# An mLSTM cell and a SwiGLU block on one core: when the third piece of the weights is asked for, where the second pair's first state is summed, and who rounds block 1

## The chip, the cores and the metric

The kernel runs on one core of a Trainium2 chip. The metric is the device time of one execution in microseconds (us). The engines are PE (TensorE, with its weight loads written PEld), DVE (VectorE), ACT (ScalarE), POOL (GpSimd) and SP (SyncE). SP and ACT issue the DMAs: those of SP appear in the profile as queue q1, those of ACT as q10, and both are served by the core's 16 DMA engines.

## The reference, cut to what matters

Inputs have 4 batches, 8 heads, 768 tokens and 40 features. The cell's output, 3072 tokens by 320, goes through a gated feed-forward block with 1536 hidden features. The three weight matrices are float64 in memory.

```python
for t in range(S):
    m_new = np.maximum(f_gate[:, :, t] + m, i_gate[:, :, t])
    f_stab = np.exp(f_gate[:, :, t] + m - m_new)
    i_stab = np.exp(i_gate[:, :, t] - m_new)
    m = m_new
    C = f_stab * C + i_stab * np.einsum('bhd,bhe->bhde', vt, kt)
    n = f_stab * n + i_stab * kt
    y[:, :, t] = o * (C @ qt) / np.maximum(np.abs(n @ qt), 1.0)
...
g = x @ w_gate
silu = g * (1.0 / (1.0 + np.exp(-g)))
return (silu * (x @ w_val)) @ w_out
```

## The kernel before, in words

**Tiling.** The tokens are cut into six chunks of 128 per batch; a chunk of all four batches is a group of 512 tokens. The cell runs chunk by chunk in matrix form: scores, weights, values, and a state `C` carried on. Heads come in two halves P = 0 and P = 1 (two batches each). For the first chunk the weights of all heads lie in `W0`, which is a view of the first eight slots of `h_sb`, the 13-slot ring that later holds the hidden features (512 words a slot); batch u uses slots 2u and 2u + 1.

**Feed-forward.** For group g, `hidden(g, m)` makes block m of the 12 blocks of 128 hidden features: PE multiplies the gate and the value weights (line 648, 20 products in the profile) into two PSUM banks of tag "gen" (four banks in all, so two blocks are in flight), ACT takes Silu of the first (line 653), and DVE multiplies by the second into slot `(12g + m) mod 13` of `h_sb` (line 654). A block can only start on PE when DVE has finished line 654 of the block before the last. `project` then multiplies by the output weights.

**Weights.** They are float64 and arrive as pairs of 32-bit words, in ten pieces (`piece_load`, line 165): pieces 0 and 1 hold block 0 and block 1, pieces 2 to 6 two blocks each, pieces 7 to 9 the output weights. A piece of gate and value weights has a gate half, issued by SP, and a value half, issued by ACT for pieces 0 to 4 and by SP after that. A piece waits in a buffer: one of two `raw` buffers, or a tile that is free at the time ("home"). Block j is converted in three steps: `scale(j)`, two ACT operations (lines 190 and 192: `top`, `low`); `join(j)`, two DVE operations (lines 199 and 200); and `rounded(j)`, one integer addition on POOL or on DVE (line 207).

**Order.** Every engine runs its instructions in the order in which the kernel writes them. The opening part is written out by hand (`first_...`, lines 564 to 611), with `burn` issuing constant bfloat16 products on PE. Then a table `slots` says what runs after each block m of group 0, and a table `ahead` which blocks are converted inside `hidden(0, m)`, after its products have been issued and before its Silu. Blocks 9 to 11 are rounded by DVE, all others but block 0 by POOL.

**What the change touches.** In the opening: `sig(0)` and `sig(1)` (Sigmoid of the output gates, line 463), `piece_load(2)` into slots 8 to 12 of `h_sb`, `piece_load(3)` into `wo_sb`, `burn(6)`, `piece_load(4)` into a `raw` buffer, `first_state(0)`, `convert(1)` and the Exp of `step1` (line 609). In the group's table: `first_state(1)` (PE line 552, 32 products, and a copy into `C`, line 121) and the loads of the next `k` and `q` after block 0; `piece_load(6)` after block 1.

**What lies further down the same queues.** After block 2 SP issues `weights_load(1)`: two loads of the running maxima `M_dram` into `w_sb` (line 447). After block 6 come `weights_sub(1, P)` on DVE (line 451), which reads `w_sb`, and `weights_mask` on POOL (line 456). Inside `hidden(0, 7)`, block 10 is converted and rounded on DVE, before DVE's line 654 of block 7.

Of the kernel before, what the change touches and what calls it, by code (L numbers as in the profile page):

```python
# [13 lines left out]
AF = mybir.ActivationFunctionType  # L14
# [10 lines left out]
def kernel(  # L25
# [18 lines left out]
    nc = tc.nc  # L44
# [7 lines left out]
    D1 = D + 1  # L52
# [4 lines left out]
    NKC = DM // HP  # L57
    UH = BH // 2
    UA = UH // 2
    NH = NFC + 1  # L60
# [15 lines left out]
    def bank(name, tag="cell"):  # L76
        return psum.tile([128, 512], F32, name=name, tag=tag)

    def half(i):
        return slice(i * SUB, (i + 1) * SUB)  # L80
# [5 lines left out]
    def heads(P):  # L86
        return slice(P * UH, (P + 1) * UH)

    k_sb = const.tile([128, BH, DP], F32)
    q_sb = const.tile([128, BH, DP], F32)  # L90
# [10 lines left out]
    wo_sb = const.tile([128, NFC, DM], F32)  # L101
    h_sb = const.tile([128, NH, TW], F32)
# [16 lines left out]
    def copy(eng, dst, src):  # L119
        if eng is nc.scalar:  # L120
            nc.scalar.copy(dst, src)
        else:
            eng.tensor_copy(dst, src)
# [16 lines left out]
    def piece_load(p, home=None):  # L140
        kind, m, n = PIECES[p]
        if kind == "gv":
            a, d = NKC, n * 128
            src = [(slice(i * HP, (i + 1) * HP), w[:, m * 128:(m + n) * 128].rearrange("(c p) f -> p c f", p=HP))
                   for i, w in enumerate((moe_w_gate, moe_w_val))]
            queues = (nc.sync, nc.scalar if p < 5 else nc.sync)
        else:
            a, d = n, DM
            src = [(slice(0, 128), moe_w_out[m * 128:(m + n) * 128].rearrange("(a p) d -> p a d", p=128))]
            queues = (nc.sync,)  # L150
        if src[0][1].dtype == F32:
            for r, w in src:
                if kind == "o":
                    nc.sync.dma_start(out=wo_sb[r, m:m + n, :], in_=w)
                else:
                    for x in range(n):
                        nc.sync.dma_start(out=wgv_sb[r, m + x], in_=w[:, :, ts(x, 128)])
            return
        if home is None:
            raw = conv.tile([128, 4 * NKC * 128], U32, name="raw")  # L160
        else:
            raw = home.rearrange("p a t -> p (a t)").bitcast(U32)
        raw = raw[:, 0:2 * a * d]
        for (r, w), queue in zip(src, queues):
            queue.dma_start(out=raw[r].rearrange("p (a d) -> p a d", a=a), in_=w.bitcast(U32))
        words = raw.rearrange("p (a d two) -> p a d two", two=2, a=a)
        raws[p] = (words[:, :, :, 0], words[:, :, :, 1])
        split(p)
# [4 lines left out]
    def split(p):  # L173
        if p in raws:
            lo, hi = raws.pop(p)
            kind, m, n = PIECES[p]
            if kind == "gv":
                for c in range(n):
                    r = slice(c * 128, (c + 1) * 128)
                    blocks[m + c] = (lo[:, :, r], hi[:, :, r], wgv_sb[:, m + c])  # L180
            else:
                for c in range(0, n, 2):
                    blocks[NFC + (m + c) // 2] = (lo[:, c:c + 2], hi[:, c:c + 2], wo_sb[:, m + c:m + c + 2, :])

    def scale(j):
        if j in blocks:
            lo, hi, dst = blocks[j]
            a, d = hi.shape[1], hi.shape[2]
            top = conv.tile([128, NKC * 128], F32, name="top", bufs=1).rearrange("p (a d) -> p a d", a=a)
            nc.scalar.mul(top, hi.bitcast(F32), 2.0 ** -112)  # L190
            low = conv.tile([128, NKC * 128], I32, name="low").rearrange("p (a d) -> p a d", a=a)
            nc.scalar.mul(low, lo, 2.0 ** -29)
            blocks[j] = (low, top.bitcast(U32), dst)

    def join(j):
        if j in blocks:
            lo, top, dst = blocks[j]
            both = dst.bitcast(U32)
            nc.vector.tensor_scalar(both, top, scalar1=3, scalar2=None, op0=ALU.logical_shift_left)
            nc.vector.scalar_tensor_tensor(both, in0=top, scalar=0x80000000, in1=both, op0=ALU.bitwise_and,  # L200
                                           op1=ALU.bitwise_or)
            blocks[j] = (lo, dst.bitcast(I32))
# [6 lines left out]
    def convert(j, eng=None):  # L209
        scale(j)  # L210
        join(j)
        rounded(j, eng)
# [10 lines left out]
    warm = early.tile([128, 1], F32)  # L223
# [35 lines left out]
    step1 = keep1  # L259
# [81 lines left out]
        eng.tensor_tensor(vw_sb[:, heads(P)], v_sb[:, heads(P)], w_sb[:, heads(P), last].to_broadcast([128, UH, D1]),  # L341
                          op=ALU.mult)

    def small(name, n=UA):
        return bank(name)[:, 0:n * D1].rearrange("p (a d) -> p a d", d=D1)

    def add(n, P):
        ps = [small("add") for _ in range(2)]
# [8 lines left out]
    def state(s):  # L357
        return C_ring[s % 3]
# [103 lines left out]
    def sig(P):  # L462
        nc.scalar.activation(o_sb[:, heads(P)], o_sb[:, heads(P)], AF.Sigmoid)


    def burn(n, tag="cell"):
        t = bank("burn", tag)
        for _ in range(n):
            nc.tensor.matmul(t, lhsT=junk[:, 0:128], rhs=junk, start=True, stop=True)
# [4 lines left out]
    A, V, G = nc.scalar, nc.vector, nc.gpsimd  # L474
# [52 lines left out]
    def first_own(u):  # L527
        first_y[u] = bank("first_y", "gen")[:, 0:H * D1].rearrange("p (h d) -> p h d", d=D1)
        for h in range(H):
            nc.tensor.matmul(first_y[u][:, h, :], lhsT=W0[:, u * H + h, :], rhs=v_sb[:, u * H + h, :], start=True, stop=True)  # L530
# [13 lines left out]
            nc.vector.tensor_tensor(x, x, o_sb[:, u * H:(u + 1) * H], op=ALU.mult)  # L544
        nc.gpsimd.tensor_copy(x_sb[:, 2 * P:2 * P + 2, DM:], x_sb[:, 2 * P:2 * P + 2, 0:HP])

    def first_state(P, eng):
        ps = small("add")
        for a in range(UA):
            for two in range(2):  # L550
                h = P * UH + 2 * a + two
                nc.tensor.matmul(ps[half(two), a, :], lhsT=k_sb[:, h, :], rhs=vw_sb[:, h, :], start=True, stop=True)
        copy(eng, state(2)[:, P * UA:(P + 1) * UA], ps)

    def first_seam(P, engs):
# [30 lines left out]
    first_scores(1)  # L586
    first_x(1)
    sig(0)
    sig(1)
    piece_load(2, h_sb[:, NH - NKC:])  # L590
    piece_load(3, wo_sb)
    burn(3)
    first_own(2)
    first_own(3)
    first_gate(0)
    first_x(2)
# [1 line left out]
    first_seam(0, (A, A, V))  # L598
    scale(0)
    first_gate(1)  # L600
    burn(6, "gen")
    piece_load(4)
    join(0)
    first_seam(1, (A, A, V))
    rounded(0, V)
    first_state(0, A)
    late_decay()
    convert(1)
    nc.scalar.activation(step1, step1, AF.Exp)
    piece_load(5)  # L610
    nc.sync.dma_start(out=M_dram, in_=flat(M_sb))

# [104 lines left out]
    def load_all(dst, a, n):  # L717
# [3 lines left out]
    run = lambda f, *a: (lambda: f(*a))  # L721


    on_vector = (9, 10, 11)
    ahead = {m: [m + 2] for m in range(4)}
    ahead.update({4: [6], 5: [7, 8], 6: [9], 7: [10], 8: [11], 9: [], 10: [], 11: []})
    slots = {
        0: [run(first_state, 1, A), run(load_all, k_sb, k, 1), run(load_all, q_sb, q, 1)],
        1: [run(piece_load, 6, h_sb[:, NH - NKC:]), run(decay_rows)],
        2: [run(late_turns), run(weights_load, 1), run(load_all, v_sb, v, 1)],  # L730
        3: [run(decay)],
        5: [run(turn, 0, (A, A), (A, V))],
# [44 lines left out]
    for g in range(1, NG):  # L777
        n, f = g + 1, g + 2
# [67 lines left out]
```

## Time and profile before

| | |
|---|---|
| three runs, median (lowest to highest) | 554.49 us (554.26 to 555.3) |
| the profiled execution | 555.16 us |
| its span, first to last instruction | 553.0 us |
| PE busy in the span | 546.4 us |
| DVE, ACT, POOL busy | 234.4, 134.7, 106.6 us |
| granted TensorE clock | 1.00 throughout |
| DMA moved | 45.69 MB, mean 83 GB/s; 190 GB/s in the first 60 us |

The table's times are of one profiled execution except for the first row. The profile lists instructions by source line with start and duration, the wait before each and what ended it, and it follows the chain of work that ended last back from the end. PE's busy time is modelled from pipelined products, so where PE looks busy it need not run at its peak; where it stands, it shows.

### The profile page before, as it was taken

What the parts mean: (1) busy time and instruction counts of PE and PEld (TensorE: products, weight loads), DVE (VectorE), ACT (ScalarE), POOL (GpSimd) and SP (SyncE); (2) the same over time, 40 slices, a digit from 0 to 9 for tenths busy, and PEclk for the clock granted to TensorE, in tenths of its full rate; (3) what the DMA queues carried; (4) which work ended last, traced back from release to release, by engine and by line L of the source; (5) the groups of instructions that cost most, each with busy time, mean ns of one, the idle gap of its engine ahead of it and who ended that gap; (6) DMA issues with size and microseconds to landing.
All of it is one profiled execution on the core that took longest, in us unless ns stands there. A gap on an engine that the chain in (4) does not pass through costs nothing.

```text
span 553.0 us, 11595 instructions
## 1 busy us (share of the span) xinstructions
PE 546.4 (99%) x4992; PEld 312.9 (57%) x4992; DVE 234.4 (42%) x394; ACT 134.7 (24%) x202; POOL 106.6 (19%) x97
## 2 busy tenths in 40 slices
PE   8999999999999999999999999999999999999997
PEld 4955546675545575544576455466455567444475
DVE  5956687962156332445521445531426621011100
ACT  4366564443101033110124101005110100111100
POOL 2314355574011151011133001114001200000000
PEclk9999999999999999999999999999999999999999
DMA  9999996798631763660464451395000131000000
GB/s 125 177 280 187 192 274 115 155 111 125 68 49 17 108 109 83 71 76 5 82 127 104 53 68 27 49 149 107 13 1 2 29 62 43 12 1 0 2 24 24
DMA packets 223994, 45.69 MB, mean 83 GB/s; under 512 B 214504, under 2 KB 219112, under 8 KB 223944
## 3 DMA queue, kind: packets, MB, share of 16 engines
q1 hardware_dynamic: 222036, 42.11, 46.7%
q10 hardware_dynamic: 1908, 2.85, 2.0%
q8 instruction: 39, 0.64, 0.5%
q14 instruction: 11, 0.09, 0.1%
HBM read 35.68 MB, written 4.01 MB: 72 GB/s over the span
## 4 chain that ended last, share of the span: by engine, by line
PE 92%; DMA 4%; SPq 3%; POOL 0%; DVE 0%; ACT 0%; issue 0%; ACTq 0%; POOLq 0%
PE gv_ps L648 55%; PE o_ps L664 24%; PE o_ps L671 5%; SPq L117 3%; DMA h_sb<-in_moe_w_val_dram 2%; PE inter L377 2%; PE sp L331 2%; PE intra L382 2%; DMA o_sb<-in_o_gate_dram 2%; PE add L353 1%; PE tp_kq L296 0%; POOL wgv_sb L207 0%; PE tp_x L439 0%; DVE wgv_sb L200 0%; ACT top L190 0%
## 5 line engine op out<-in xcount | busy, mean ns | idle before, releaser
L648 PE MATMUL gv_ps<-xT,wgv_sb 64*128 64x512 f32 x1440 | 317.3, 593 | 1.6 <-POOL wgv_sb L207 1.1
L648 PEld LDWEIGHTS gv_ps<-xT,wgv_sb 64*128 64x128 f32 x1440 | 139.1, 187 | 159.4 <-issue 154.6
L654 DVE TENSOR_TENSOR h_sb<-sg,gv_ps 128x512 f32<-128x512 f32 x72 | 49.5, 687 | 214.5 <-ACT sg L653 214.4
L664 PE MATMUL o_ps<-wo_sb,h_sb 128*128 128x320 f32 x480 | 130.5, 433 | 0.0
L664 PEld LDWEIGHTS o_ps<-wo_sb,h_sb 128*128 128x128 f32 x480 | 90.8, 190 | 41.0 <-issue 3.8
L653 ACT ACTIVATE sg<-gv_ps 128x512 f32<-128x512 f32 x72 | 43.0, 597 | 268.6 <-PE gv_ps L648 268.5
L362 POOL TENSOR_TENSOR C<-C,dec 128x328 f32<-128x328 f32 x20 | 14.5, 735 | 137.7 <-DVE C L369 137.6
L456 POOL TENSOR_SCALAR_AFFINE_SELECT w_sb<-w_sb 64x1024 f32<-64x1024 f32 x20 | 27.8, 1388 | 60.2 <-DVE w_sb L451 59.3
L658 ACT COPY z_sb<-o_ps 128x320 f32<-128x320 f32 x24 | 10.0, 422 | 94.7 <-PE o_ps L664 90.9
L403 POOL TENSOR_TENSOR o_sb<-o_sb,y_sb 128x640 f32<-128x640 f32 x10 | 14.3, 1428 | 79.2 <-DVE y_sb L394 79.1
L671 PE MATMUL o_ps<-wo_sb,h_sb 128*128 128x320 f32 x96 | 26.9, 437 | 0.0
L451 DVE TENSOR_TENSOR w_sb<-g_T,w_sb 128x1024 f32<-128x1024 f32 x10 | 13.2, 1355 | 27.6 <-DMA w_sb<-M_dram 27.6
L426 DVE STREAM_TRANSPOSE xT<-x_sq 128x640 f32<-128x640 f32 x16 | 12.5, 822 | 23.7 <-DMA x_sq<-x_sb 23.7
L671 PEld LDWEIGHTS o_ps<-wo_sb,h_sb 128*128 128x128 f32 x96 | 17.9, 190 | 7.2
L394 DVE TENSOR_TENSOR y_sb<-y_sb,intra 64x328 f32<-64x328 f32 x40 | 19.7, 493 | 0.8 <-PE intra L382 0.2
L369 DVE TENSOR_TENSOR C<-C,add 40x328 f32<-40x328 f32 (+1 forms) x36 | 17.7, 493 | 1.3 <-PE add L353 0.4
L207 POOL TENSOR_TENSOR wgv_sb<-wgv_sb,low 128x640 int32<-128x640 int32 x8 | 12.3, 1541 | 23.7 <-DVE wgv_sb L200 21.9
L377 PEld LDWEIGHTS inter<-C,qT 64*64 64x64 f32 x640 | 10.2, 134 | 7.3 <-issue 6.1
L341 POOL TENSOR_TENSOR vw_sb<-v_sb,w_sb 128x656 f32<-128x656 f32 x10 | 12.8, 1303 | 0.4
L338 DVE TENSOR_TENSOR w_sb<-sp,w_sb 128x512 f32<-128x512 f32 x20 | 12.7, 682 | 0.0
L460 ACT ACTIVATE w_sb<-w_sb 128x1024 f32<-128x1024 f32 x10 | 10.6, 1058 | 8.8 <-POOL w_sb L456 8.8
L397 DVE TENSOR_SCALAR den<-den 128x16 f32<-128x16 f32 x10 | 12.2, 1216 | 0.3
(129 smaller groups left out, 343.7 us busy)
## 6 DMA issues: line engine op xcount, KB each, us to landing
w_sb<-M_dram SPq DMA_DIRECT2D x10, 512.0 KB, 7.2
x_sq<-x_sb SPq DMA_DIRECT2D x128, 40.0 KB, 2.0
k_sb<-in_k_dram SPq DMA_DIRECT2D x12, 320.0 KB, 6.1
v_sb<-in_v_dram SPq DMA_DIRECT2D x12, 320.0 KB, 5.7
o_sb<-in_o_gate_dram SPq DMA_DIRECT2D x12, 320.0 KB, 5.4
raw<-in_moe_w_out_dram SPq DMA_DIRECT2D x3, 1280.0 KB, 7.8
out_dram<-z_sb SPq DMA_DIRECT2D x24, 160.0 KB, 1.8
q_sb<-in_q_dram SPq DMA_DIRECT2D x32, 64.0 KB, 2.4
```

What stands on the lines that cost most here:

```text
L117: nc.sync.dma_start(out=dst[:, heads(P), 0:D], in_=tokens(a, c, P))
L362: nc.gpsimd.tensor_tensor(state(s + 1)[:, a], state(s)[:, a], dec[:, s - 2, a].unsqueeze(2).to_broadcast([128, UA, D1]), op=ALU.mult)
L369: nc.vector.tensor_tensor(c, c, ps[r], op=ALU.add)
L377: nc.tensor.matmul(inter[two][half(i), a, :], lhsT=qT[half(two), P * UA + a, half(i)], rhs=state(2 * n + i)[half(two), P * UA + a, :], sta ...
L394: nc.vector.tensor_tensor(t, t, intra[i][half(c)], op=ALU.add)
L403: eng.tensor_tensor(o, o, y[:, :, 0:D], op=ALU.mult)
L456: nc.gpsimd.affine_select(w, w, compare_op=ALU.is_ge, fill=NEG, base=0, pattern=[[0, UH], [1, SUB]], channel_multiplier=-1)
L648: nc.tensor.matmul(ps[i], lhsT=wgv_sb[half(i), m, PAIRS[kc][i] if g < 2 else kc, :], rhs=x[half(i), kc, :], start=(kc == 0), stop=(kc == N ...
L653: nc.scalar.activation(sg, ps[0], AF.Silu)
L654: nc.vector.tensor_tensor(hid(g, m), sg, ps[1], op=ALU.mult)
L664: nc.tensor.matmul(p, lhsT=hid(g, m)[:, ts(u, L)], rhs=wo_sb[:, m, :], start=(m == 0), stop=(m == NFC - 1))
L671: nc.tensor.matmul(ps[u], lhsT=hid(g, m)[:, ts(u, L)], rhs=wo_sb[:, m, :], start=(m == 0), stop=(m == NFC - 1))
```

## The change

Piece 2's home becomes slots 1 to 5 of `h_sb`, so its load has to wait until PE has read the first chunk's weights of batch 2; it is now issued by both queues right behind `first_own(2)`, and ahead of `sig(1)` on ACT. Piece 3 moves into slots 8 to 12 and behind `burn`, piece 4 into `wo_sb` and behind `convert(1)`; pieces 5 and 6 use the `raw` buffers. The second pair's `first_state` products take the place of five of six constant products; their bank has tag "gen", and DVE copies the sum into `C`. Block 1 is rounded by DVE. A one-column Silu stands ahead of the first real one, and the Exp of `step1` moves behind block 1. Block 2 is converted behind block 0's Silu and product (in `slots[0]`) where it had been ahead of them (`ahead[0]`).

```diff
-    def small(name, n=UA):
-        return bank(name)[:, 0:n * D1].rearrange("p (a d) -> p a d", d=D1)
+    def small(name, n=UA, tag="cell"):
+        return bank(name, tag)[:, 0:n * D1].rearrange("p (a d) -> p a d", d=D1)
...
-    def first_state(P, eng):
-        ps = small("add")
+    def first_state(P, tag="cell"):
+        ps = small("add", tag=tag)
...
+        return ps
+
+    def first_kept(P, ps, eng):
         copy(eng, state(2)[:, P * UA:(P + 1) * UA], ps)
...
     sig(0)
-    sig(1)
-    piece_load(2, h_sb[:, NH - NKC:])
-    piece_load(3, wo_sb)
     burn(3)
     first_own(2)
+    piece_load(2, h_sb[:, 1:1 + NKC])
+    sig(1)
     first_own(3)
...
     first_gate(1)
-    burn(6, "gen")
-    piece_load(4)
+    ps1 = first_state(1, "gen")
+    burn(1, "gen")
+    piece_load(3, h_sb[:, NH - NKC:])
     join(0)
     first_seam(1, (A, A, V))
     rounded(0, V)
-    first_state(0, A)
+    first_kept(0, first_state(0), A)
+    first_kept(1, ps1, V)
     late_decay()
-    convert(1)
-    nc.scalar.activation(step1, step1, AF.Exp)
+    convert(1, V)
+    nc.scalar.activation(warm, warm, AF.Silu)
+    piece_load(4, wo_sb)
     piece_load(5)
...
     ahead = {m: [m + 2] for m in range(4)}
+    ahead[0] = []
...
-        0: [run(first_state, 1, A), run(load_all, k_sb, k, 1), run(load_all, q_sb, q, 1)],
-        1: [run(piece_load, 6, h_sb[:, NH - NKC:]), run(decay_rows)],
+        0: [run(convert, 2), run(load_all, k_sb, k, 1), run(load_all, q_sb, q, 1)],
+        1: [run(piece_load, 6), run(nc.scalar.activation, step1, step1, AF.Exp), run(decay_rows)],
```

## The prediction

> **What bounds the kernel now.** I read the page's first line of engines, then the chain of work that ended last, then the timeline of the first 85 us, then the DMA view by windows.
>
> ```profile
> PE 546.4 (99%) x4992; PEld 312.9 (57%) x4992; DVE 234.4 (42%) x394; ACT 134.7 (24%) x202; POOL 106.6 (19%) x97
> ```
>
> PE stands for only 6.6 us of 553.0. The end moves only if PE loses work or stands less. The chain names the one stand inside the kernel:
>
> ```profile
> 25.43 13.59 DMA h_sb<-in_moe_w_val_dram
> ...
> 41.51 1.54 POOL wgv_sb L207
> 43.05 0.04 issue
> 43.10 4.80 PE gv_ps L648 x20
> ```
>
> The value half of piece 2 is issued at 25.43 and lands 13.59 later; block 2 is converted from it, and PE waits. From 43.10 on the chain is PE without a break over 0.4 us. The timeline shows what stands around that point:
>
> ```profile
> 36.39 1.13 PE L552 MATMUL add<-vw_sb,k_sb 128*64 128x41 f32 x32
> 37.45 4.56 PE L648 MATMUL gv_ps<-xT,wgv_sb 64*128 64x512 f32 x20
> 39.17 0.80 ACT L190 ACTIVATE top<-h_sb 128x640 f32<-128x640 f32 x1 [3.66 <-DMA h_sb<-in_moe_w_val_dram]
> 40.67 1.28 ACT L653 ACT_TABLE_LOAD   x1
> 41.97 0.60 ACT L653 ACTIVATE sg<-gv_ps 128x512 f32<-128x512 f32 x1
> 43.10 4.80 PE L648 MATMUL gv_ps<-xT,wgv_sb 64*128 64x512 f32 x20 [1.08 <-POOL wgv_sb L207]
> ```
>
> The state sum sits between blocks 0 and 1 and costs PE 37.45 - 36.39 = 1.06; the wait before block 2 costs 1.08; and block 2 lasts 4.80 where block 1 lasted 4.56, since its second product waits for block 0's late line 654 (0.24).
>
> One more place decides, thirty microseconds later, on DVE:
>
> ```profile
> 70.97 1.22 DVE L451 TENSOR_TENSOR w_sb<-g_T,w_sb 128x1024 f32<-128x1024 f32 x1 [1.31 <-DMA w_sb<-M_dram]
> 72.12 0.49 DVE L199 TENSOR_SCALAR wgv_sb<-top 128x640 uint32<-128x640 uint32 x1
> 72.64 1.64 DVE L200 SCALAR_TENSOR_TENSOR wgv_sb<-top,wgv_sb 128x640 uint32<-128x640 uint32 x1
> 74.41 1.54 DVE L207 CUSTOM_DVE_ANT_0 wgv_sb<-wgv_sb,low 128x1280 uint16<-128x1280 uint16 x1
> 75.87 0.68 DVE L654 TENSOR_TENSOR h_sb<-sg,gv_ps 128x512 f32<-128x512 f32 x1
> ```
>
> DVE waits for the landing of `w_sb` (70.95) and then works without a gap until line 654 of block 7 ends at 76.55. That frees the bank into which PE writes block 9. PE's loads for block 9 begin here:
>
> ```profile
> 77.18 0.19 PEld L648 LDWEIGHTS gv_ps<-xT,wgv_sb 64*128 64x128 f32 x2 [0.24 <-issue]
> ```
>
> So PE comes to block 9 only 77.18 - 76.60 = 0.58 after its bank is free. A PE that is earlier by more than that stands, unless `w_sb` lands earlier too.
>
> **The change part by part.**
>
> *State sum in place of constant products.* The six constant products are issued from 27.50 until the next product at 28.79, 1.29 in all. The 32 state products take 0.97 from first to next issue (30.24 to 31.2), one constant product 0.22: 1.19 in the same place, between two seams, where the next product waits for DVE's line 544 until 29.04 anyway. Its values (POOL, line 501) were ready at 22.44. So block 0 still starts at 31.90 and the 1.06 between blocks 0 and 1 goes: block 1 at 36.39. No profile row shows the clock with less filler; it is granted 1.00 in every window, and the array has products either way; I take nothing. The copy into `C` on DVE is not shown in this form: 128x256 from PSUM took DVE 0.42, 128x512 0.69, so 0.42 to 0.69, nearest 0.5. It delays `late_decay` and block 1's `join` from 32.81 to about 33.3.
>
> *Block 1 rounded by DVE.* POOL ended it at 35.84; DVE's form took 0.82 at 30.94, up to 1.54 beside POOL (above). `join` would end at 34.7 and the rounding at 35.5 to 36.2, before PE's 36.39. Worth nothing, costs nothing.
>
> *Piece 2.* `first_own(2)` is the first half of the products at 22.88 (3.66 for two batches), so both halves are issued at about 24.9. On SP, pieces 3 to 5 queue behind it; piece 3 was issued at 23.69 and its data did not move before 31, so 1.3 later is free. On ACT, `sig(1)` is behind it: its gates land at 25.40, the issue takes 0.60 (24.9 to 25.5), so it starts 0.1 later, and its reader on DVE starts at 28.14. The gate half was alone on the engines between 28 and 32, and with the value half beside it later the rate was far higher:
>
> ```profile
> q1 hardware_dynamic: 410, 0.78, 105.7%
> ```
> ```profile
> DMA packets 1032, 2.02 MB, mean 336 GB/s; under 512 B 47, under 2 KB 47, under 8 KB 1032
> ```
>
> The first is 28 to 32 us (0.78 MB in 4 us, 194 GB/s, q1 alone), the second 34 to 40 (both queues). Two halves of 0.655 MB at 336 take 3.9: 28 to about 32, landed by 34 or 35 with the last engine's 2 us of delay as in the value half before (most engines 36.9, last 39.02). The conversion now stands behind block 0's Silu: PE ends block 0 at 36.46, Silu starts at 36.5 because its table is loaded already, `top` 0.49 later (as 41.97 to 42.46) at 37.0, and from `top` to PE's start it took 43.10 - 39.17 = 3.93: block 2 ready at 40.93. PE comes to it at 43.10 - 1.08 - 1.06 = 40.96. So the wait is gone, and the 0.24 with it: PE's lead is 1.06 + 1.08 + 0.24 = **2.38** when it leaves block 2. The halves may land as late as 37.0 at no cost.
>
> *Pieces 3 and 4 on ACT.* The issue of piece 3's value half takes the place of piece 4's (30.04, 0.61), piece 4's goes behind the Silu in ACT's idle time (ACT waited from 35.5 to 39.0). Piece 3 is wanted at about 43.6 now, 45.05 before; its value half landed at 42.73 then. It can be 3.5 late before block 4 (on PE at 50.7) waits.
>
> *Tables.* Before: Exp at 33.48, Silu at 40.67. After: Silu, Exp, Silu: one load more, 1.28. Block 1's Silu ends at 41.6, load to 42.9, Exp 0.74 to 43.6; PE transposes `step1` at 40.96 + 4.49 = 45.45. It is hidden with 1.8 to spare, without that cover it would cost its excess over 1.8. Between the old load and its Silu there is no more than 0.02 (40.67 + 1.28, 41.97). The Trainium skill (ScalarE: Activation LUTs, What ACT_TABLE_LOAD costs) speaks against an added switch: it counts a drain of about 1.38 on top, 2.66 in all; that would bring Exp's end to about 45.0, still 0.4 early, so the sum is the same.
>
> *Where the lead goes.* PE now reaches block 9 at 77.18 - 2.38 = 74.8. Its bank is free 5.65 after `w_sb` lands. Does `w_sb` land earlier? SP issues it at 56.61, in a row of DMAs that has no gap for SP: the second `k` load takes SP from 39.53 to 50.06, the two `w_sb` loads 56.61 to 65.74. These are the DMA engines filling up, not waits for PE (all their readers and writers are done). From 24.1 to 46.5 q1 always has work, and after the change it has the same bytes in the same order: five halves of pieces 2 to 5 on q1, three halves on q10. Shared time is 3 x 0.655 MB / 0.168 = 11.7; the rest of q1, 3.28 - 1.97 MB, at 194 takes 6.8; together 18.5, whichever half goes first, as long as q1 is never left standing. So asking for the halves together brings piece 2 forward and brings `w_sb` nothing: 70.95, give or take 0.5 for instruction fetches and the slowest engine. Lead kept: **0.58**, the rest is a new wait of PE at block 9 of about 1.8. After it, block 10 starts at 83.0 against a bank free at 82.1, and nothing else is nearer than 1 us. The price of the unknown `w_sb` shift is one for one: 0.08 to 1.08 gained.
>
> The Trainium skill (DMA: Bandwidth & Descriptors, Queues, rings and completion order) says each DMA engine goes round-robin between queues with work. The 28 to 32 window disagrees: q10 held piece 2's value half since 26.03 and moved nothing. Were it round-robin from the start, the halves would already share and the bytes, and so `w_sb`, would again be where they are.
>
> **Sum.** The profiled execution took 555.16 with a span of 553.0, 2.16 around it; its span would become 552.4. Against the median of the runs shown, 554.49, the same 0.58 gives **553.9**.
>
> **Rivals.**
> *The whole lead arrives* (0.22): `w_sb` lands 1.8 or more earlier, or partly so. For it: between 49 and 51 the DMA engines are nearly idle while SP's `k` load waits for the slowest of them; were that gap closed, 1.3 come. Against it: the slowest engine itself has no gap. 554.49 - 2.38 = 552.1 at the best, 552.1 to 553.3 as a class.
> *A value half pushes its gate half back* (0.13, the slower side): both are asked for at one moment, and if q10 goes first, alone, q1 stands. For it: piece 1's value half ran from 22.9 to 24.1 with q1 silent. Price: piece 2's value half alone takes 0.655 / 0.194 = 3.4 and only two halves share: 3.4 + 7.8 + (3.28 - 1.31) / 0.194 = 21.4 against 18.5, so `w_sb` is up to 2.9 late, and block 9 up to 2.3 later than before: 554.5 to 556.8. It decides as soon as `w_sb` lands after 71.53.
> *The change does not do what it says* (0.05): piece 2 lands after 39 again, or ACT is held by an issue's wait. The lead shrinks, but down to 0.58 block 9 takes it anyway: 553.9 to 554.5.
>
> **How the numbers follow.** My forecast, the lead capped at block 9, has 0.60: 553.4 to 554.4. The range reaches to the whole lead below and into the slow rival above, 552.1 to 555.2, leaving about 0.15 out. 0.2% is 1.11 us, about what a measurement of this kernel can tell from no change. Faster by more than that: the whole-lead class and the edge of my forecast, 0.25; slower by more: most of the second rival, 0.11; within: 0.64.
>
> **What would show it.** Right: no `add` products between blocks 0 and 1; block 2 starts at about 41 without a wait on POOL; blocks 3 to 8 about 2.4 earlier; `w_sb` lands at 70.5 to 71.5; PE waits 1.8 for DVE's line 654 before block 9, and from there all is 0.6 earlier. Wrong: block 9 at 75 without a wait (`w_sb` early), or at over 77.2 (`w_sb` late).

## The result and the profile after

The changed kernel took a median of 557.23 us in five executions (556.35 to 557.81), the kernel before 554.5 beside it: the ratio on record is 1.0039, 95% interval 1.0021 to 1.0056 (the bare quotient of the medians is 1.0049). Forecast were 553.9 and a range up to 555.2, so it is slower where I expected a small gain. The same kernel, timed again later in twelve executions, took 555.89 against 555.08: 1.0011 (0.9993 to 1.0029). The loss is thus between nothing and half a per cent; the gain of 0.58 us did not come in either timing.

The profiled execution of after took 556.59 with a span of 554.25, 1.21 more than the 553.04 of before and 1.8 more than the 552.4 of the forecast. The page's first line of engines:

```profile
PE 547.5 (99%) x4987; PEld 317.6 (57%) x4987; DVE 236.1 (43%) x396; ACT 136.0 (25%) x203; POOL 105.3 (19%) x96
```

PE has 1.1 us more busy time with five products fewer (4987 for 4992). Three places matter for the time. In all timelines the columns are start, duration, engine and line, with the wait before in brackets; lines 653, 658 and 659 of after are 648, 653 and 654 of before.

**First, the clock.** The windows view of after, 26 to 30 us (window, length, busy time and count of PE, PEld, DVE, ACT, POOL, then granted clock, DMA share, GB/s):

```profile
26.00:30.00 4.00, 4.00 (x39) 3.67 (x40) 2.69 (x11) 2.18 (x4) 0.29 (x1) 0.57 1.11 201
```

The granted clock is 0.57 here, where the profile of before had 1.00 throughout: it was 0.5 from 26.20 to 29.61, a stretch of 3.41. The transposes (line 564) and the state sum run at half speed in the PE timeline of after:

```profile
26.83 2.37 PE L564 MATMUL tp_x<-ident,x_sb 128*128 128x128 f32 x10
29.13 1.34 PE L552 MATMUL add<-vw_sb,k_sb 128*64 128x41 f32 x32
30.40 0.39 PE L469 MATMUL burn<-junk 128*128 128x512 bf16 x1
30.63 1.32 PE L564 MATMUL tp_x<-ident,x_sb 128*128 128x128 f32 x10
...
33.29 13.53 PE L653 MATMUL gv_ps<-xT,wgv_sb 64*128 64x512 f32 x60 [0.28 <-DVE wgv_sb L207]
46.75 0.49 PE L627 MATMUL tp_g<-ident,i_sb 32*128 32x32 f32 x5
```

Ten transposes took 2.37 before the sum and 1.32 after it. Block 0 starts at 33.29, 1.39 later than before (31.90). The stretch begins ahead of the place that the change touches: the constant products that it removed ran from 27.50 to 28.79 in before, and up to there PE's order of work is the same. Then the change does what it says: blocks 0, 1 and 2 are one piece of sixty products without a sum or a wait between them. PE leaves block 2 at 46.75 where it was 47.83: a lead of 1.08, which is the 2.38 of the prediction, and 0.1, less 1.39.

**Second, block 9.** DVE's timeline of after:

```profile
71.33 1.22 DVE L451 TENSOR_TENSOR w_sb<-g_T,w_sb 128x1024 f32<-128x1024 f32 x1 [2.75 <-DMA w_sb<-M_dram]
72.47 0.48 DVE L199 TENSOR_SCALAR wgv_sb<-top 128x640 uint32<-128x640 uint32 x1
73.00 1.64 DVE L200 SCALAR_TENSOR_TENSOR wgv_sb<-top,wgv_sb 128x640 uint32<-128x640 uint32 x1
74.77 1.54 DVE L207 CUSTOM_DVE_ANT_0 wgv_sb<-wgv_sb,low 128x1280 uint16<-128x1280 uint16 x1
76.23 0.68 DVE L659 TENSOR_TENSOR h_sb<-sg,gv_ps 128x512 f32<-128x512 f32 x1
```

The same five instructions as before, 0.36 later, and DVE waits for `w_sb` 2.75 instead of 1.31. PE's loads stand behind the last of them:

```profile
76.96 0.30 PEld L653 LDWEIGHTS gv_ps<-xT,wgv_sb 64*128 64x128 f32 x4 [0.67 <-DVE h_sb L659]
```

This is the new wait that was forecast, and it comes at the forecast place. The scores after it start at 81.45 (before: 81.56): 0.1 of the lead is left.

**Third, a stand at 100 us that I had not counted.** PE timeline, before and then after:

```profile
100.98 0.67 PE L382 MATMUL intra<-v_sb,w_sb 64*64 64x41 f32 x30 [0.33 <-issue]
```
```profile
99.81 0.78 PE L382 MATMUL intra<-v_sb,w_sb 64*64 64x41 f32 x40
102.28 0.56 PE L382 MATMUL intra<-v_sb,w_sb 64*64 64x41 f32 x24 [1.70 <-issue]
```

"issue" means that the profile shows nothing that PE waited for. PE stops in the middle of 64 equal products and goes on at 102.28 instead of 100.98, 1.30 late; the span ends 1.21 later. The forecast had 100.4 here, so the 1.9 between it and the trace is all in this stand: whatever block 9 left of the lead ends in it. What comes late is found among the transfers. The DMA view of after, 99 to 99.9 and 99.9 to 101 us (queue and kind: packets, MB, share of 16 engines):

```profile
q1 hardware_dynamic: 128, 0.30, 84.2%
```
```profile
q8 instruction: 1, 0.02, 5.7%
q1 hardware_dynamic: 9, 0.01, 2.1%
```

And of before, 98.3 to 99.5:

```profile
q8 instruction: 1, 0.02, 5.6%
q1 hardware_dynamic: 14, 0.01, 2.9%
```

One instruction block of 16 KB on q8 moves at 99.92, just as the packets of piece 9 (1280 KB, or 1.31 MB, on q1) run out. Before, it moved at 98.34, at the same point of piece 9 (5.25 and 5.29 after piece 9's issue). PE goes on 2.36 after the block's start here, 2.64 in before, and 2.28 to 2.6 in the other profiles below that have the stand; where PE comes to this product 2.85 or more after the block's start, there is none. By the times, then, piece 9 sets the block and the block sets PE; the profile names neither wait. Why piece 9 is later shows in SP's timeline, before and after:

```profile
70.42 2.37 SPq L165 DMA_DIRECT2D raw<-in_moe_w_out_dram  x2
72.89 8.42 SPq L117 DMA_DIRECT2D o_sb<-in_o_gate_dram  x2
82.65 10.34 SPq L315 DMA_DIRECT2D q_sb<-in_q_dram  x16
93.09 0.43 SPq L165 DMA_DIRECT2D raw<-in_moe_w_out_dram  x1
```
```profile
70.59 6.02 SPq L165 DMA_DIRECT2D raw<-in_moe_w_out_dram  x2
76.66 5.50 SPq L117 DMA_DIRECT2D o_sb<-in_o_gate_dram  x2
83.01 11.52 SPq L315 DMA_DIRECT2D q_sb<-in_q_dram  x16
94.63 0.43 SPq L165 DMA_DIRECT2D raw<-in_moe_w_out_dram  x1
```

The first row is pieces 7 and 8. SP holds them 6.02 instead of 2.37, and piece 8 goes out at 76.24 where it was 72.25. The change moved pieces 4 and 6 between the homes and the two `raw` buffers: these now take pieces 0, 1, 5, 6, 7, 8, 9 in turn, where they took 0, 1, 4, 5, 7, 8, 9. Piece 8 therefore follows piece 6 in its buffer, and piece 6 is read until ACT has converted block 11 (`low`, to 76.2). The `o` loads, the sixteen `q` loads and piece 9 queue behind it; piece 9 is issued 1.54 later: the `q` loads start 0.36 later and hold SP 1.18 longer.

### The profile page after: what moved, and what is told of

The parts are those of the page before. It is cut to its first block, busy times and chain, and to the rows that moved or that the text cites. A ratio compares the mean times of both kernels' runs of the same rounds, so it can differ in the third digit from the quotient of the medians.

```text
span 554.3 us, 11586 instructions
## 1 busy us (share of the span) xinstructions
PE 547.5 (99%) x4987; PEld 317.6 (57%) x4987; DVE 236.1 (43%) x396; ACT 136.0 (25%) x203; POOL 105.3 (19%) x96
## 3 DMA queue, kind: packets, MB, share of 16 engines
q10 hardware_dynamic: 1908, 2.85, 2.0%
## 4 chain that ended last, share of the span: by engine, by line
PE 98%; DVE 1%; issue 0%; ACT 0%; POOL 0%; ACTq 0%; POOLq 0%; DVEq 0%
PE gv_ps L653 56%; PE o_ps L669 23%; PE o_ps L676 5%; PE inter L377 2%; PE sp L331 2%; PE intra L382 2%; PE add L353 1%; PE first_y L530 1%; PE burn L469 1%; PE tp_x L564 1%; PE tp_kq L509 1%; PE sp L519 1%; PE wps L480 0%; PE tp_kq L296 0%; PE wps L484 0%
## 5 line engine op out<-in xcount | busy, mean ns | idle before, releaser
L653 PEld LDWEIGHTS gv_ps<-xT,wgv_sb 64*128 64x128 f32 x1440 | 142.9, 187 | 155.9 <-issue 150.1
L207 POOL TENSOR_TENSOR wgv_sb<-wgv_sb,low 128x640 int32<-128x640 int32 x7 | 10.8, 1539 | 22.5 <-DVE wgv_sb L200 22.5
L382 PE MATMUL intra<-v_sb,w_sb 64*64 64x41 f32 x640 | 11.5, 227 | 1.7 <-issue 1.7
```

The lines of the kernel that those rows point to most:

```text
L382: nc.tensor.matmul(intra[i][half(c), a, :], lhsT=w_sb[half(i), h, :], rhs=v_sb[half(i), h, :], start=True, stop=True)
L653: nc.tensor.matmul(ps[i], lhsT=wgv_sb[half(i), m, PAIRS[kc][i] if g < 2 else kc, :], rhs=x[half(i), kc, :], start=(kc == 0), stop=(kc == N ...
```

## The experiments

Two readings stood against each other. One: the loss is on the DMA side, piece 8's buffer delays piece 9 and the instruction block (theory C from the second round on; "rival B" of the first round is the DMA side too, with `w_sb` and block 9 as the place). The other: the change removed five products, so PE's instruction stream and clock stand elsewhere, and that makes both the stretch at half clock at 26 us, "the dip", and the stand at 100 (theory A of the first round; in after_sub_late the letter A stands for the wait at block 9). Each ratio below is against the kernel before on the same chip.

**Filler put back (first round).**

```diff
# after_burn6 (before_burn1 is the reverse edit on before)
-    burn(1, "gen")
+    burn(6, "gen")
# after_small5; in before_small5 it replaces burn(6, "gen")
-    burn(1, "gen")
+    burn(1, "gen", 5)      # five products of 8 columns behind one of 512
```

> The changed kernel with six constant products again behind the moved state sum (PE has as many instructions as before, and the array its filler). Theory A (two costs come from the five removed products: the place in PE's instruction stream at which a 16 KB block of instructions is fetched moves by ten instructions, so that PE stands 1.70 us at the cell's products near 100 us instead of 0.33; and with less filler the granted clock falls to half for 3.4 us windows in the opening): the stand falls back to about 0.3, the clock stays at 1.00, and the time falls from 557.2 to 554 to 555.2, although PE is given 1.1 us more work. Rival B (the time comes from the DMA side: w_sb lands later and block 9 waits): nothing changes, 557.2, or 558.3 with the added work.

> The changed kernel with one constant product of 512 columns and five of 8 columns, which keep PE's instruction count of before but hardly occupy the array. Theory A: the fetch stand near 100 us falls from 1.70 to about 0.3, the dip of the clock stays (0.994 to 0.997 over the run in most executions): 557.2 - 1.4 = 555.8, between 555.0 and 556.5. Rival B: unchanged, 557.2.

> The kernel before with one constant product in place of six and nothing else changed. Theory A: it takes on both costs without the change's gains: the stand near 100 us grows from 0.33 to about 1.7 and the clock dips in most executions, 1.0 to 1.5 each with no lead to swallow them: 554.5 + 1.4 + 0 to 1.5 = 555.9 to 557.4. Rival B: filler is filler, no change: 554.5, or less by the time the filler took, if that was on the path.

> The kernel before with one constant product of 512 columns and five of 8 columns in place of six of 512. Theory A: the instruction count is kept, so no stand near 100 us beyond 0.3; only the clock can dip: 554.5 to 556.0, with executions at a clock of 1.000 at 554.5. Rival B: 554.5.

Measured: after_burn6 1.0037 (1.0014 to 1.0061), after_small5 1.0022 (1.0003 to 1.0040), before_burn1 1.0011 (0.9998 to 1.0025), before_small5 0.9998 (0.9982 to 1.0014). The wait lists of PE, of after, after_small5 and before_small5 (total, times, longest):

```profile
PE intra L382 <- issue: 1.7, 1, 1.7
```
```profile
PE intra L382 <- issue: 2.4, 1, 2.4
```
```profile
PE intra L382 <- issue: 0.9, 1, 0.9
```

With the instruction count of before restored, the stand is 1.52 (after_burn6) and 2.36 (after_small5); with fewer products in before it does not grow (0.33 in before_burn1). In all four PE resumes 2.36 to 2.59 after the q8 block's start. Theory A falls for the length of the stand. The count of instructions sets its place, though: PE stops after 34 or 35 of the 64 products in the five profiles with as many constant products as before, after 39 or 40 in the eight with five fewer. As for the dip, in the profile of after_burn6 the clock is 1.00 for the whole span and block 0 starts at 32.61, but PE then waits 0.9 at block 9, scores start at 81.83, and nothing is gained: lead won in the opening is lost at block 9. The profiled execution of before_burn1 is of little use: a load of the opening landed late (block 0 at 34.38, `w_sb` at 74.75), and it took 558.77 with a median of 555.91.

**The queue behind piece 8 (second round).**

```diff
# after_p6_home, slot 1
-run(piece_load, 6)
+run(piece_load, 6, h_sb[:, NH - NKC:])
# after_p9_first: slot 10 loses load_squares, slot 11 ends with it
-run(rounded, 12), run(load_squares, q_sq, q, 2)]
+run(rounded, 12)]
-run(piece_load, 9)]
+run(piece_load, 9), run(load_squares, q_sq, q, 2)]
# after_sub_late: from slot 6 to the head of slot 7
-run(weights_sub, 1, 0), run(weights_mask, 0), run(piece_load, 7)]
+run(piece_load, 7)]
-7: [run(weights_sub, 1, 1), ...
+7: [run(weights_sub, 1, 0), run(weights_mask, 0), run(weights_sub, 1, 1), ...
# after_all3: the three together
```

> The changed kernel with piece 6 in slots 8 to 12 of h_sb, as before the change, so that piece 8 takes a buffer that is free early. Theory C (the change makes piece 8 wait for block 11's conversion, 72.25 to 76.24; the loads behind it on SP, piece 9 last, are 1.5 us late; PE's next instructions come through the same DMA engines behind piece 9, and PE stands 1.70 us for them near 100 us): piece 8 is issued at 70 to 73, piece 9 at about 93, the stand falls to 0.3 to 0.9, and the time by 0.8 to 1.4, to between 0.3 below and 0.6 above the kernel before. Rival D (the stand comes from where PE's own instruction blocks end): the stand stays at 1.5 or more, the time at 2 to 2.5 above before.

> The changed kernel with piece 9 asked for ahead of the sixteen q loads, not behind them. Theory C: piece 9 is issued at about 90.2, is through by 96, and PE's instruction block is no longer behind it: no stand near 100 us (0 to 0.3), the time 1.4 to 1.7 lower than the changed kernel's. Rival D: the stand stays.

> The changed kernel with the subtraction and mask that wait for w_sb moved behind block 7's product on DVE. Theory A (block 9 is held by DVE's wait for w_sb): PE no longer waits at block 9 and comes to the scores at about 80.4, not 81.45. Theory C on top of it: piece 9 does not come earlier, so the stand near 100 us grows by about as much, to 2.2 to 2.7, and the time moves by less than 0.4. Rival (nothing but block 9 holds the lead): 1.0 faster than the changed kernel.

> All three edits together: piece 6 in h_sb, piece 9 ahead of the q loads, the subtraction behind block 7's product. If block 9's bank and the fetch behind piece 9 are the two places where the lead of 2.4 goes, the whole lead and the 0.33 of before reach the end: 1.5 to 2.7 below the kernel before (0 to 1.5 below if the clock dips in the opening). Rival (a third place takes it): no faster than before by more than 0.5.

Measured: after_p6_home 1.0304 (1.0268 to 1.0339) and after_all3 1.0410 (1.0373 to 1.0447). In both, piece 6 goes over piece 3 before blocks 4 and 5 are converted from there, so those two blocks are made of piece 6's words, and PE stands 16.9 and 17.4 for them at 52 us. Their results are wrong, and of the theory they tell nothing.

after_p9_first: 1.0062 (1.0036 to 1.0087), slower than the change itself. The stand near 100 is gone (piece 9 issued at 90.33, block on q8 at 97.08), as theory C says, but all sixteen `q` loads now come behind piece 9, and its wait list shows what they cost:

```profile
PE gv_ps L653 <- ACT z_sb L663: 3.6, 1, 3.6
```

A wait of 3.6 at 131.5 us; only after_all3 has one like it (2.7). I did not follow it to its cause.

after_sub_late: 0.9983 (0.9957 to 1.0009). DVE's first `w_sb` subtraction now stands behind the product of block 7 instead of ahead of it:

```profile
72.68 0.69 DVE L659 TENSOR_TENSOR h_sb<-sg,gv_ps 128x512 f32<-128x512 f32 x1 [0.89 <-ACT sg L658]
73.28 2.35 DVE L451 TENSOR_TENSOR w_sb<-g_T,w_sb 128x1024 f32<-128x1024 f32 x2
```

`w_sb` landed at 71.44 here, later than in after, but block 7's product ends at 73.4 instead of 76.9 and PE does not wait at block 9: scores start at 80.53. That settles the cap at block 9. The stand is 1.42 at 101, shorter than the 2.2 to 2.7 that theory C gave it, since piece 8 went out at 74.05 and piece 9 at 93.35, both earlier than in the change. So the order on DVE, which frees buffers, and SP's queue are not independent.

**Piece 6's buffer and the state sum (third round).**

```diff
# after_p6_slot2: blocks 4 and 5 converted earlier, piece 6 to its old home one slot later
+    ahead[2], ahead[3] = [4, 5], []
-1: [run(piece_load, 6), run(nc.scalar.activation, ...
+1: [run(nc.scalar.activation, ...
-2: [run(late_turns), ...
+2: [run(piece_load, 6, h_sb[:, NH - NKC:]), run(late_turns), ...
# after_p6_sub: this and after_sub_late
# before_state: on before
-    burn(6, "gen")
+    ps1 = first_state(1, "gen")
+    burn(1, "gen")
-    first_state(0, A)
+    first_kept(0, first_state(0), A)
+    first_kept(1, ps1, V)
-    convert(1)
+    convert(1, V)
# after_no_state: on after, the reverse for the sum
-    ps1 = first_state(1, "gen")
-    burn(1, "gen")
+    burn(6, "gen")
-    first_kept(1, ps1, V)
-0: [run(convert, 2), ...
+0: [lambda: first_kept(1, first_state(1), A), run(convert, 2), ...
```

> The changed kernel with piece 6 in slots 8 to 12 of h_sb, asked for behind block 2 (blocks 4 and 5 are both converted inside block 2, so that piece 3 is out of these slots). Piece 8 then takes piece 5's buffer, free since 65, not piece 6's. Theory C (piece 8's buffer makes the loads behind it on SP late, piece 9 last, and PE's instruction block comes behind piece 9): piece 8 is issued by 73, piece 9 at about 93, PE's stand near 100 us falls from 1.70 to 0.3 to 0.9, the time by about 1, to 0.5 to 1.5 above before. Rival (piece 9 is late for another reason): piece 8 early, but piece 9 still at 94.6 and the stand at 1.5 or more.

> The same with the subtraction and mask behind block 7's product. The subtraction alone left 1.42 of the stand and came out level with before (ratio 0.998). If piece 8's buffer is the second place, this one reaches the scores 1 earlier and piece 9 is out of the way at about the same time relative to PE: 0.5 to 2 below before. If piece 9 only follows the q loads, whose start the mask sets, the stand stays near 1.4 and the time level with before.

> The kernel before with the part of the change that lies on PE and DVE alone: the second pair's state sum in place of five constant products, its copy and block 1's rounding by DVE; loads, tables and order of conversion as before. Theory A: the 1.06 between blocks 0 and 1 goes, but block 2's weights still arrive at 43.1, so PE waits there for 2.1 and not 1.1; the clock dips in the opening in some executions, which that wait swallows in part: 0 to +1 on before. Theory that this part carries a gain: 0.5 to 1 faster.

> The changed kernel with the state sum back behind block 0 and the six constant products back: loads, tables and order of conversion alone. Theory C: the clock holds at 1.00, the lead at block 2 is 1.3 and block 9's bank takes all over 0.6; piece 9 is as late as in the changed kernel, so PE stands 1.5 to 2 near 100 us: 0.5 to 1.5 above before. If the filler and the clock carry the loss: level with before or up to 0.6 faster.

Measured: after_p6_slot2 1.0012 (0.9996 to 1.0028); after_p6_sub 0.9993 (0.9976 to 1.0010); before_state 1.0006 (0.9992 to 1.0021); after_no_state 1.0018 (1.0002 to 1.0034).

With piece 6 out of the `raw` buffers piece 8 goes out at 72.24 and 72.09, as before, but piece 9 only at 93.72 and 93.42, and the stand stays at 1.25 and 1.51. So piece 8's buffer can explain some 0.9 of piece 9's delay, not all of it, and after_p6_sub is not the 0.5 to 2 below before that was expected. The state sum with the rounding on DVE changes nothing measurable in before, although the profile of before_state has the dip (26.17, block 0 at 33.29): scores start at 80.68, and the stand is 0.33. So the state sum is not where the loss lies, and in before's order it gains nothing. after_no_state, with the loads, tables and order of conversion alone, is slower as expected (0.5 to 1.5 above before). Its profiled execution, of 559.81, shows what the slow rival of the prediction describes: SP, late since piece 1 (gate half asked for at 24.94, in after at 20.24), asked for piece 2's gate half 1.0 after ACT had asked for the value half; from 28 to 30 q10 moved 0.40 MB and q1 0.01; the value half landed at 31.65, the gate half at 37.01, `w_sb` at 73.69, and PE waited 2.63 at block 9.

**Piece 9 between the halves of the `q` loads (fourth round).**

```diff
# after_p9_mid, before_p9_mid
-    def load_squares(dst, a, c):
-        for two in range(2):
+    def load_squares(dst, a, c, twos=(0, 1)):
+        for two in twos:
...
-run(rounded, 12), run(load_squares, q_sq, q, 2)]
+run(rounded, 12), run(load_squares, q_sq, q, 2, (0,))]
-run(piece_load, 9)]
+run(piece_load, 9), run(load_squares, q_sq, q, 2, (1,))]
# after_w_first: after_p6_slot2, in slot 2
-run(piece_load, 6, h_sb[:, NH - NKC:]), run(late_turns), run(weights_load, 1), ...
+run(weights_load, 1), run(piece_load, 6, h_sb[:, NH - NKC:]), run(late_turns), ...
# after_p6_sub_p9: after_p6_sub and after_p9_mid
```

> The changed kernel with piece 9 asked for between the two halves of the q loads, not behind both. If PE's instructions come late because they stand behind piece 9: piece 9 is issued at about 90.3 and through by 96.5, the stand near 100 us is 0.3 or less, and the time is 1 to 1.7 below the changed kernel's: level with before to 1 above. If not: the stand stays at 1.5 or more.

> The kernel before with piece 9 between the two halves of the q loads. If PE's instructions stand behind piece 9: the stand of 0.33 (0.3 to 0.9 in the runs of this kernel's kin) goes, 0.3 to 0.6 faster, about the edge of what five rounds tell. If not: no change.

> The changed kernel with the two loads of w_sb asked for ahead of piece 6 (which stands in h_sb, behind block 2). If block 9 follows w_sb at 5.65: w_sb lands at 64 to 65, block 9 is not held by it; it is held by block 10's conversion instead, which now waits for piece 6 until about 72 and stands ahead of block 7's Silu, so that the scores start at about 80 in place of 81.4: 1 to 2.5 below the changed kernel, with the stand near 100 us at 0.3 to 1.5. If w_sb only happens to land near: scores at 81.1 or later.

> Piece 6 in h_sb behind block 2, the subtraction and mask behind block 7's product, piece 9 between the halves of the q loads. If block 9's bank and the block of instructions behind piece 9 are the two places: no wait at block 9, no stand near 100 us, 1.2 to 2.5 below the kernel before, less 1.4 in executions in which the clock dips in the opening (then level to 1 below).

Measured: after_p9_mid 0.9987 (0.9972 to 1.0002), before_p9_mid 0.9984 (0.9967 to 1.0001), after_w_first 0.9994 (0.9976 to 1.0012), after_p6_sub_p9 0.9971 (0.9951 to 0.9992). SP's and then PE's timeline of after_p9_mid:

```profile
83.15 6.24 SPq L315 DMA_DIRECT2D q_sb<-in_q_dram  x8
90.25 0.38 SPq L165 DMA_DIRECT2D raw<-in_moe_w_out_dram  x1
```
```profile
99.91 1.13 PE L382 MATMUL intra<-v_sb,w_sb 64*64 64x41 f32 x64
```

Piece 8 is as late as in the change (76.38), scores are held at block 9 as in the change (81.58), the dip is there (27.35); only piece 9 is earlier by 4.4. The 64 products run through without a stand, the q8 block having moved at 97.02. With that one edit the change is level with before or a little better. This is the cleanest evidence on the loss: it is in the stand at 100, and piece 9's place in SP's queue sets it. But the same edit makes before as fast (before_p9_mid has no stand either), so the change's own lead is worth nothing measurable even then: in this profile block 9 takes it.

after_w_first brings `w_sb` itself forward: it lands at 64.16 (71.31 in after), and DVE's timeline has no wait for it any more, but one for ACT:

```profile
68.76 1.22 DVE L451 TENSOR_TENSOR w_sb<-g_T,w_sb 128x1024 f32<-128x1024 f32 x1
72.98 0.49 DVE L199 TENSOR_SCALAR wgv_sb<-top 128x640 uint32<-128x640 uint32 x1 [3.00 <-ACT top L190]
...
75.21 0.68 DVE L659 TENSOR_TENSOR h_sb<-sg,gv_ps 128x512 f32<-128x512 f32 x1
```

Scores start at 80.74, 47.23 after block 0, which is the distance of the kernels without a wait at block 9 (47.22 in after_sub_late, 47.21 in after_p6_sub). Two independent edits, then, remove the cap, one by the order on DVE and one by the landing. Neither beats before while the stand is left: 1.36 here.

after_p6_sub_p9 removes both caps: no wait at block 9, block 7's product done at 72.4, piece 9 issued at 89.36, no stand. Its PE timeline at 97.91, where before resumes at 100.98:

```profile
97.91 1.13 PE L382 MATMUL intra<-v_sb,w_sb 64*64 64x41 f32 x64
```

This profiled execution had no dip, a span of 550.9, and a median of 553.87: the only one so far whose interval lies below the kernel before. Before with these two edits was not run, so how much of this gain is the change's lead is not shown; the interval overlaps that of before_p9_mid. PE does wait before block 2 here:

```profile
PE gv_ps L653 <- POOL wgv_sb L207: 0.7, 1, 0.7
```

Without the dip block 0 starts at 31.76, and piece 2, whose value half lands at 37.34, is late again.

**The changed kernel again, and the best with filler (last round).**

```diff
# after_again: the changed kernel as it is
# best_burn: on after_p6_sub_p9
     sig(1)
+    burn(3)
     first_own(3)
```

> The changed kernel itself, timed beside the experiments. Theory (the loss is the stand behind piece 9, with block 9 taking all but 0.1 to 0.6 of the lead): 1.5 to 2.5 above before, ratio 1.003 to 1.0045; in the profile, scores 10.1 after w_sb lands and a stand of 1.4 to 2.4 near 100 us. If the first timing was chance: below 1.002.

> The kernel with all three edits and three more constant products (0.65 us of PE) between first_own(2) and first_own(3). If the clock's dip in the opening costs it 1.4 in most executions: the clock stays at 1.00, 0.3 to 1 faster than without, about 2 below before. If the dip is rare there or the products delay the seam as much as they save: level with it or up to 0.7 slower, 0.5 to 1.5 below before.

Measured: after_again 1.0011 (0.9993 to 1.0029), less than the 1.003 to 1.0045 expected. In its profiled execution `w_sb` landed at 69.61 (71.31 in the first), scores started at 80.51, piece 8 went out at 74.54, piece 9 at 92.97 and the stand was 1.15, to 100.76 (1.4 to 2.4 were expected):

```profile
100.76 0.56 PE L382 MATMUL intra<-v_sb,w_sb 64*64 64x41 f32 x24 [1.15 <-issue]
```

So one kernel's `w_sb` varies by 1.7 between executions, and so does what block 9 takes: nothing here, since scores start 47.22 after block 0. PE comes to the scores 1.05 ahead of before, and the q8 block is not late (98.18, before 98.34). Yet PE goes on at 100.76, where before goes on at 100.98: the stand alone takes 0.8 of the lead.

best_burn: 553.37 against 555.08, 0.9968 (0.9952 to 0.9984), with all twelve executions from 552.82 to 554.32. Its ratio is level with that of after_p6_sub_p9, so a gain in time from the filler is not shown; both beat the kernel before. What it does to the clock is shown by the mean granted clock, which is on record for every execution (one stretch of 3.41 at half makes it 0.997): at least 0.999 in all twelve of best_burn, 0.997 in six of the eleven of after_p6_sub_p9, whose median is 554.07 against 553.22 for the other five.

## Why the prediction was wrong

**The opening.** Right: the sum between blocks 0 and 1 and the 0.24 went, block 1's rounding cost nothing, and the tables and pieces 3 and 4 delayed nobody. Mis-sized: piece 2. I let both halves share 336 GB/s from 28 on and land by 34 or 35. The DMA view of after, 30 to 32 us:

```profile
DMA packets 225, 0.43 MB, mean 214 GB/s; under 512 B 16, under 2 KB 16, under 8 KB 225
q10 hardware_dynamic: 146, 0.30, 71.1%
q1 hardware_dynamic: 79, 0.13, 35.0%
```

The value half on q10 moved nothing before 30, and then the two queues together had 214, not 336. The gate half landed at 32.36, the value half at 37.37, past the 37.0 that I allowed. In after, block 2 did not wait only because block 0 was late itself; with block 0 at 31.76 the wait is 0.74 (above), and in after_small5, with block 0 at 31.35, it is 1.11. In such executions the 2.38 were not to be had in whole.

The wait of 1.08 before block 2 was itself that of one execution: it is 0.30 in before_p9_mid and under 0.25 in before_small5, whose loads in the opening are those of before. (Block 4 would have started at 53.52 - 2.38 = 51.1, not at 50.7; nothing hung on it.)

The clock: "granted 1.00 in every window" rested on one execution. A dip delays block 0 by 1.39 in after. Of the profiles with the sum and without the five products, ten of thirteen were granted 0.5 for 3.41 us from 26.2 to 27.4 on (best_burn, with three more further ahead, was not); of the four with all six wide products, none. But these stretches begin before 27.50, where the products stood, so that their absence there can't have set them off; before_small5 and before_burn1 lack them and have no dip at 26 to 28; and 80 of the 149 executions of before that were timed beside the experiments have a mean clock of 0.997 or less, as have 10 of the 17 of the changed kernel. Where in those executions the clock fell is not on record. So that the change brings the dip is not shown, and "I take nothing" is not refuted. In after the dip probably did not decide the time, since PE, had it come earlier, would have stood longer at 100 (the q8 block moves at 100.00 in after_burn6, which has no dip, and at 99.92 in after); in after_again the six executions with a mean clock of 0.997 or less have a median of 556.5, the other six 555.5, so elsewhere it may have. The Trainium skill (TensorE: Matmul & The Clock Gate, Part 1) tells of a free-running activity window of about 3.4 us and of two clocks, half and full; this case's stretch of 3.41 at 0.5 agrees.

**The cap at block 9.** Right: place, cause and the landing of `w_sb` (71.31 where 70.5 to 71.5 was said). after_sub_late and after_w_first show it, each by its own way: with the cap gone, scores keep their distance of 47.2 to block 0 (as in after_again, where `w_sb` came early by itself). The lead kept there was 0.1 and not 0.58, mostly because `w_sb` came 0.36 later; that is within the half microsecond I gave it.

**"Nothing else is nearer than 1 us."** This is the step that failed. The chain of before and its list of waits show PE stopping for 0.33 at 100.65. I called the chain "without a break over 0.4 us" and passed over it, so the sum put the cost of this stand at nothing. It took all of the lead that block 9 had left: PE went on at 102.28 where the forecast has 100.4. Before comes to this product 2.31 after the q8 block's start, where 2.28 to 2.64 was seen to be needed: it has no time in hand there. If it is the block that PE waits for, no lead gets past this point unless the block comes earlier, and a delay of the block is paid in full. The two profiles of the changed kernel show both: with the block at 98.18, as in before, a lead of 1.05 at the scores shrinks to 0.22; with the block 1.58 late, PE goes on 1.30 late. (The stand is 0.33 in before, before_burn1 and before_state alike, so this may be the least that a block just too late costs, and not the exact shortage.) I followed the change's moved DMAs as far as `w_sb`, not to the end of SP's queue: the exchange of buffers between pieces 4 and 6 gives piece 8 another predecessor, 4 us later, and in this execution piece 9 and the block on q8 come 1.5 later. The three rivals had no place for this. The slower one ("a value half pushes its gate half back") did not happen in the two profiles of the changed kernel, but it did in that of after_no_state, which has the same loads: `w_sb` at 73.69, within the "up to 2.9" late, and the span 4.5 above before. How many of the slow executions of the changed kernel it explains is open.

**How much is settled.** Shown: the stand goes with piece 9's position (present in every profile that has piece 9 behind all `q` loads, but for after_p6_home, where PE is 17 late anyway; absent in the six that have it further ahead, of which after_all3 tells little, since there too PE is 17 late), and moving piece 9 alone brings the change to 0.9987, below the interval of its first timing and level with before. Shown in part: that piece 8's buffer makes piece 9 late; undoing it alone gave 1.0012 beside the change's own 1.0039 and 1.0011, which can't be told apart, and brought back 0.9 of piece 9's 1.54; but piece 9 was issued at 92.97 in after_again with piece 8 at 74.54, and at 94.84 in after_w_first with piece 8 at 72.86, so piece 8 is not all that sets it. Inferred from the times, and from the stand's fixed place in PE's count of instructions: that PE waits for the block on q8, and the block for piece 9's packets, since the trace shows when it moves and not what waits for it. Open: the size of the loss, 0.4% in one timing and 0.1% in another; the landing of `w_sb` moved from 69.6 to 71.3 between two executions of the same kernel, and no run here pins that down.

## What to carry to other kernels

A short stand of the bounding engine can be a fixed point with no time in hand: before you count a lead, follow it through every such stand up to the end of the kernel, and ask what it waits for, above all where the profile names no releaser. When a buffer rotation is changed, list the new predecessor of every later user; the load that is held may be several transfers behind the ones you edited, and all that queue behind it on the same issuing engine are late with it. When a lead is won early and two caps stand behind it, removing one of them can show nothing; here only the two kernels that removed both gained more than the measurement can miss. And where the clock or a landing differs between executions of one kernel, one profile is not enough to lay a difference to the change.

## What the runs showed of the hardware

PE seems to stop for its own instructions: one 16 KB block on queue q8 moved late beside the 1.31 MB of piece 9 on q1, and PE, in the middle of 64 products of 64x41, went on 2.28 to 2.64 us after that block began to move. The stop came after 34 or 35 of the products, or after 39 or 40 where five constant products fewer had gone before.

A stand of PE of 2.36 to 3.56 us was followed by a stretch of 3.41 at half clock in all five profiles that have one (after_small5, after_no_state, after_p9_first, after_all3, before_burn1); the stretch began between 0.1 before and 1.2 after PE went on. None of the eleven stands of 1.0 to 1.7 was followed by one. So a low mean clock may be what a stand leaves behind, and not only a cause of lost time.

Half clock comes without a stand, too: in ten profiles it began between 26.17 and 27.35 although PE, with products of 128x41 and transposes of 128x128 in float32, had stood nowhere for more than 0.1 since 18 us. In best_burn, with three more constant bfloat16 products of 128x512 from 24.35 on, no execution of twelve had a mean clock below 0.999. Six of the eleven of after_p6_sub_p9, without them, had 0.997. What decides in which execution it comes stays open.
